# Attention and a low-rank mixer on one core: finer loads and another order for batch 0, narrower unread matmuls, V loaded once, V of batch 1 ahead of the last quarter of w2

## The chip, the core and the metric

The kernel runs on one core of a Trainium2 chip. A core has five engines that run beside each other and meet at semaphores: TensorE (PE: matmuls, and PEld, its loads of weights), VectorE (DVE), ScalarE (ACT), GpSimd (POOL) and SyncE (SP). POOL and SP also issue transfers (DMAs), which 16 DMA engines carry out. SBUF is the working memory of 128 partitions, PSUM the memory that matmuls write. The metric is the time of one execution in microseconds (us) of the device, as the median of several runs. A profile comes from one execution; its "span" is from the first instruction to the last, and the execution's time has some 1.7 us more around it.

## The reference

Sliding-window causal attention (each query sees itself and the 63 positions before it) over 8 batches, 8 heads, 576 positions and 64 elements a head, and after it a mixer: a low-rank mix over the positions (U and V of rank 32) added to the attention's output, then a two-layer MLP with relu, and u added again.

```python
scores = scale * np.matmul(q, k.transpose(0, 1, 3, 2))
rel = pos[:, None] - pos[None, :]
mask = (rel >= 0) & (rel < 64)
scores = np.where(mask, scores, -1e9)
attn = softmax(scores)
x = np.matmul(attn, v)            # to (8, 576, 512)
h = x.transpose(0, 2, 1) @ U @ V
u = x + h.transpose(0, 2, 1)
out = u + np.maximum(u @ w_ch1, 0.0) @ w_ch2
```

All inputs and the output are float32 in memory; the kernel computes in bf16 with float32 sums.

## The kernel before, in words

The order on every engine is the order in which the program's text issues instructions; it is written out by hand.

**Two kinds of work, interleaved.** The MLP runs over 9 chunks of 512 tokens (`mlp(c)`). Each chunk has 32 slots: slots 0 to 15 are one feature tile each of the first layer (`ch1`, line 655: 4 matmuls of 128x512, relu on DVE or ACT), slots 16 to 31 are one token tile and a quarter of the sum each of the second layer (`ch2`, line 678: 4 matmuls of 128x512; after the last quarter DVE adds u, line 687, and SP writes the tile out, line 690). In chunk 0 the second layer goes by pairs of token tiles, quarter by quarter. Attention of batch c+1 is cut into pieces that are put behind certain slots of chunk c, by the tables `PLACE`, `PLACE_0` to `PLACE_3`:

- T: transposes of keys and queries. Batches 0 and 1 use PE (line 274) with a copy from PSUM (`TK` and `TQ`, lines 285 and 290). From batch 2 on SP transposes them by DMA (`TX`, line 296), ten for a batch, at the slots of `CROSS`.
- S: scores of a pair of heads, and the exp on ACT (line 357); a last one (`SC8`, tiles `low` and `high` from batch 2 on) takes the last block of all heads.
- M: the mask, as a product. In batch 0 the mask is added by PE before the scores instead (B, line 327).
- SV: shifted copies of the values (`shift_high`, `shift_low`), from tile `vA` to tile `vB`.
- PV: probabilities times values (line 399), with a division on DVE.
- U, V: the low-rank mix (lines 498 and 506; line 577), and u in bf16 (line 590). For V there is `vrep`, a bf16 copy of the matrix V that stands four times on 32 partitions each.
- UT: u transposed for the MLP (tile `uTc`), by PE (line 609) for batches 0 to 2 and by SP's DMA (line 605) from batch 3 on.

**Batch 0 ahead of everything.** Before chunk 0 there is nothing to interleave with, so batch 0's attention is written out piece by piece in the string `order`. Ahead of it and between its pieces stand matmuls on a tile `idle` whose result nobody reads (`turn_over`, line 749): 56 of 96 columns, and five of 512 columns.

**Transfers.** POOL's queue issues, in this order: keys and queries of batch 0 (heads 0 to 3, then 4 to 7), the values of batch 0 (`load_v(0)`), w1 in two halves, keys and queries of batch 1, w2's first two quarters, the values of batch 1, w2's last two quarters, keys and queries of batch 2. Between them stand POOL's own instructions: masks, and shifted copies that wait for values. A transfer waits for the one issued eight before it. Later, `held` (line 869) makes POOL wait for batch 2's transposes before it loads the values of batch 2 and the keys and queries of batch 3. SP's queue issues U and V, then the transposes and the outputs.

Of the kernel before, what the change touches and what calls it, by code (L numbers as in the profile page):

```python
# [12 lines left out]
FP32 = mybir.dt.float32  # L13
# [3 lines left out]
def kernel(  # L17
# [11 lines left out]
    nc = tc.nc  # L29
    B, H, S, D = q.shape  # L30
    DM = H * D
    R = moe_U.shape[1]
    F = moe_w_ch1.shape[1]
    P = nc.NUM_PARTITIONS
    W = 64
# [3 lines left out]
    NFC = F // P  # L39
# [6 lines left out]
    NFULL = S // P  # L46
    CH = 512
# [18 lines left out]
    ps_tp = ctx.enter_context(tc.tile_pool(name="ps_tp", bufs=1, space=bass.MemoryType.PSUM))  # L66
    first = ExitStack()
    psum = {
        "mm": first.enter_context(tc.tile_pool(name="ps_t0", bufs=2, space=bass.MemoryType.PSUM)),
        "spare": first.enter_context(tc.tile_pool(name="ps_s0", bufs=1, space=bass.MemoryType.PSUM)),  # L70
    }

    ctx.enter_context(tc.manual_schedule())
# [6 lines left out]
    w2b = const.tile([P, NFC, DM], BF16, name="w2b")  # L80
# [1 line left out]
    uf = [const.tile([P, NT, R], FP32, name=f"uf{i}") for i in range(2)]  # L82
    ub = [const.tile([P, NT, R], BF16, name=f"ub{i}") for i in range(2)]
    vrep = const.tile([P, W + S + W], BF16, name="vrep")
    vf = const.tile([P, S], FP32, name="vf")
    idle = const.tile([P, CH], BF16, name="idle")
    xs = [const.tile([P, NT, H, D], BF16, name=f"xs{i}") for i in range(2)]
    vA = [const.tile([P, NFULL, H, VW], BF16, name=f"vA{i}") for i in range(2)]
# [17 lines left out]
    def load_kq(b, split):  # L106
        grouped = b < NGR
        if grouped:
            kb, qb = (
                r[0:GP, :].rearrange("p (h c d) -> p h c d", h=H, c=GR) for r in (kr[b % 2], qr[b % 2])  # L110
            )
        else:
            kb, qb = kn[b % 2], qn[b % 2]
        loaded[b] = (kb, qb)
        if grouped:
            for h0, h1 in ((0, 4), (4, 8)) if split else ((0, H),):
                hs = slice(h0, h1)
                for t, src in ((kb, k), (qb, q)):
                    nc.gpsimd.dma_start(
                        out=t[:, hs, :, :].rearrange("p h c d -> p h (c d)"),  # L120
                        in_=src[b, hs, :, :].rearrange("h (p c) d -> p h (c d)", c=GR),
                    )
                    yield
        else:
            for t in range(NT):
                rows = P if t < NFULL else W
                for dst, src in ((kb, k), (qb, q)):
                    nc.gpsimd.dma_start(  # L128
                        out=dst[0:rows, t, :, :],
                        in_=src[b, :, t * P : t * P + rows, :].rearrange("h p d -> p h d"),  # L130
                    )
                yield

    def load_v(b):
        va, vb = vA[b % 2], vB[b % 2]
        for t in range(NFULL):
            nc.gpsimd.dma_start(  # L137
                out=va[:, t, :, 0:D],
                in_=v[b, :, t * P : (t + 1) * P, :].rearrange("h p d -> p h d"),
            )  # L140
            if t == NFULL - 1:
                nc.gpsimd.dma_start(
                    out=vb[0:W, t, :, 0:D],
                    in_=v[b, :, (t + 1) * P : (t + 1) * P + W, :].rearrange("h p d -> p h d"),
                )
# [10 lines left out]
    def shift_high(b, copy, t):  # L156
        copy(out=vB[b % 2][W:P, t, :, :], in_=vA[b % 2][W:P, t, :, :])

    def shift_low(b, copy, t):
        copy(out=vB[b % 2][0:W, t, :, :], in_=vA[b % 2][0:W, t + 1, :, :])  # L160
# [14 lines left out]
        channel_multiplier=1,  # L175
    )
    nc.vector.memset(maskA[:, 0, 0:2, :], 1.0)
    for _ in kq0:
        pass


    for n, base, step, mult in ((0, 0, 1, -1), (1, -1, -1, 1), (1, W, 1, -1)):
        nc.gpsimd.affine_select(
            out=maskA[:, 0, n, :],
            in_=maskA[:, 0, n, :],
            compare_op=ALU.is_ge,
            fill=0.0,
            base=base,
            pattern=[[step, W]],
            channel_multiplier=mult,  # L190
        )
    for i in range(2):
        nc.vector.memset(vA[i][:, :, :, D:VW], 1.0)
        nc.vector.memset(vB[i][:, :, :, D:VW], 1.0)
# [16 lines left out]


    def load_low_rank():
        for part in (vf[:, 0:1], uf[1][:, 0, :], uf[1][:, 1, 0:1]):
            nc.vector.memset(part, 0.0)
        for g in range(4):
            nc.sync.dma_start(out=vf[g * R : (g + 1) * R, :], in_=moe_V[:, :])
        nc.sync.dma_start(out=uf[1][W:P, 0, :], in_=moe_U[0:W, :])
        nc.sync.dma_start(
            out=uf[1][:, 1:NT, :], in_=moe_U[W:S, :].rearrange("(c p) r -> p c r", p=P)  # L220
        )

    w1v = moe_w_ch1.rearrange("(c p) n -> p c n", p=P)
    for lo, hi in ((0, 1024), (1024, 2048)):
        nc.gpsimd.dma_start(out=w1b[:, :, lo:hi], in_=w1v[:, :, lo:hi])
    for t in range(2):
        shift_high(0, nc.gpsimd.tensor_copy, t)
        shift_low(0, nc.gpsimd.tensor_copy, t)
    shift_low(0, nc.gpsimd.tensor_copy, 2)
    for _ in load_kq(1, False):  # L230
        pass
    w2v = moe_w_ch2.rearrange("(i p) m -> p i m", p=P)
    for i in range(0, NFC, 4):
        if i == NFC // 2:
            load_v(1)
        nc.gpsimd.dma_start(out=w2b[:, i : i + 4, :], in_=w2v[:, i : i + 4, :])

    u_tiles = {}
    uT_tiles = {}
# [7 lines left out]
    def attention(b, spare=False):  # L247
# [14 lines left out]
        def tr(src, j, wide=False):  # L262
            if spare and turn[0] % 3 != 0:
                tpb = psum["mm"].tile([P, 2 * CH], BF16, name="tpm", tag="mm")
                tp = tpb[:, 0:S].rearrange("d (c p) -> d c p", c=GR)
            elif wide:
                tpw = ps_big.tile([P, 2, 2 * CH], BF16, name="tpw", tag="big")
                tp = tpw[:, 0, 0:S].rearrange("d (c p) -> d c p", c=GR)
            else:
                tp = ps_tp.tile([P, GR, GP], BF16, name="tpg", tag="tp")  # L270
            turn[0] += 1
            for c in range(GR):
                for g in range(2):
                    nc.tensor.transpose(  # L274
                        tp[g * D : (g + 1) * D, c, :], src[:, 2 * j + g, c, :], ident[0:GP, 0:GP]
                    )
            return tp.rearrange("d c p -> d p c")

        def place_of(f, j):
            return f[j].rearrange("d (p c) -> d p c", c=GR)  # L280

        def TK(j):
            def f():
                copy = nc.vector.tensor_copy if spare and j == 2 else nc.scalar.copy
                copy(out=place_of(kt, j), in_=tr(kb, j))
            return f

        def TQ(j):
            def f():
                nc.vector.tensor_copy(out=place_of(qt, j), in_=tr(qb, j, b == 1))  # L290
            return f

        def TX(t):
# [237 lines left out]

        def idle_turns(n):
            cols = P if opened else CH
            for _ in range(n * (CH // cols)):
                nc.tensor.matmul(
                    bank(0)[:, 0:cols],
                    idle[:, 0:P],
                    idle[:, 0:cols],
                    start=not opened,
                    stop=not opened,  # L540
                )
# [104 lines left out]
    def mlp(c):  # L646
# [60 lines left out]
    }  # L707
    PLACE_0 = {"V": [0, 0, 1, 2, 2, 3, 4, 4]}
    PLACE_1 = {
        "T": [10, 10, 11, 11, 12, 12, 13, 13],  # L710
        "S": [11, 12, 13, 14, 15],
        "M": [12, 13, 14, 15, 16],
        "SV": [16, 16, 17, 17],
        "PV": [18],
        "U": [23],
        "V": [24, 25, 26],
        "UT": [27, 28, 29, 30, 102],
    }
    PLACE_2 = {
# [12 lines left out]
        "PV": [10],  # L732
        "U": [16],
        "V": [18, 19, 20],
        "UT": [19, 19, 20, 20, 21],
    }
    CROSS = {
        0: {2: [16, 17, 18, 19, 20]},
# [5 lines left out]

    unread = psum["spare"].tile([P, CH], FP32, name="unread", tag="spare")

    def turn_over(n, cols=CH):
        for _ in range(n):
            nc.tensor.matmul(
                unread[:, 0:cols], idle[:, 0:P], idle[:, 0:cols], start=True, stop=True  # L750
            )


    turn_over(56, 96)
    att = {0: attention(0, spare=True)}
    a = att[0]
    nc.vector.tensor_scalar(
# [22 lines left out]
        nc.vector.tensor_copy(out=mask[:, 7, :], in_=mask[:, 1, :])  # L780

    repeat(nc.scalar.copy, maskB)
    order = "K0 K1 B0 B1 Q0 Q1 S0 S1 K2 K3 B2 Q2 B3 Q3 S2 S3 B4 S4"
    for what in order.split():
        j = int(what[1])
        if what[0] in "SB":
            a[what[0]][j]()
        else:
            a["T"][2 * j + (what[0] == "Q")]()
        if what == "Q1":  # L790
            load_low_rank()
        turn_over({"B1": 1, "Q1": 1, "S1": 1, "B2": 1, "Q3": 1}.get(what, 0))
    nc.scalar.copy(out=ub[0][:], in_=uf[0][:])
    for t in range(2, NFULL):
        shift_high(0, nc.scalar.copy, t)
    nc.scalar.copy(out=vrep[:, W : W + S], in_=vf[:])
    for t in range(NT + 2):
        if t < NT:
            a["PV"][t]()
        if 2 <= t < NFULL + 2:  # L800
            a["XT"][t - 2]()
            a["U"][t - 2]()
        elif t == 1:
            a["idle"](1)
    for f in [a["U"][NT - 1]] + a["X3"] + a["HT"]:
        f()
    repeat(nc.vector.tensor_copy, maskA[:, 0])
# [100 lines left out]
```

The softmax here doesn't subtract the row's maximum and nothing guards it: scores larger than these inputs give would overflow.

## Time and profile before

| | us |
|---|---|
| median of 4 runs (lowest to highest) | 318.74 (318.58 to 319.21) |
| the profiled execution | 318.89 |
| its span | 317.2 |
| PE busy | 306.3 |
| DVE busy | 163.0 |
| ACT busy | 109.5 |
| POOL busy | 97.9 |
| first matmul of the MLP starts | 23.43 |
| one 128x512 matmul of the MLP, as listed (they overlap) | 0.379 |
| one exp of a pair of heads, 128x1024 | 1.03 |
| POOL's transfers: packets, MB | 100096, 18.36 |
| SP's transfers: packets, MB | 51744, 20.77 |

A busy time is the union of an engine's instructions. Matmuls are pipelined, so that four of 128x512 take some 0.87 us together although one is listed with 0.379 us. In a list of waits, a line is: who waited, for whom, us in total, how often, the longest. In a list of instructions in order of time a line is: start, us, engine, line, operation, output from inputs, shapes, count, and in brackets the idle time before it with what ended it. In a table by stretches a line is: the stretch, its length, the busy time of PE, PEld, DVE, ACT and POOL with their counts, the granted clock of PE, the share of the DMA engines, and GB/s. The landing of a transfer is given as the time from its issue.

### The profile page before, as it was taken

Reading aid. Unit: us, or ns where it says so; the run is one execution under the profiler, and the core shown is the slowest. Engines: PE = TensorE matmul, PEld = TensorE weight load, DVE = VectorE, ACT = ScalarE, POOL = GpSimd, SP = SyncE. Lnnn points to the kernel's source line nnn. Section 1 sums busy time; section 2 is a strip of 40 time slices with the busy share of each in tenths; the row PEclk is TensorE's granted clock in tenths of the full one; section 3 lists DMA queues with packets and bytes.
Section 4 is the critical chain, followed back from the end, with each engine's and each line's share of the span. In section 5 each row is a group of like instructions: output and inputs, shape, how many; then the busy total and the mean of one; then the engine's idle time right before and its main releaser. Section 6 shows DMA issues by size and latency. Waiting matters only on the chain.

```text
span 317.2 us, 6876 instructions
## 1 busy us (share of the span) xinstructions
PE 306.3 (97%) x2856; PEld 149.2 (47%) x2856; DVE 163.0 (51%) x297; ACT 109.5 (35%) x176; POOL 97.9 (31%) x127
## 2 busy tenths in 40 slices
PE   7889999999998999899999999999999999999995
PEld 6544554544454544354445444544454444444442
DVE  4464558428655955575557455745474443016011
ACT  3555670358126620444034503450345003201500
POOL 8671273169735354442544460000000000000000
PEclk9999999999999999999999999999999999999999
DMA  7999999999999999999999999955100520020011
GB/s 111 159 222 205 187 176 126 138 163 196 125 137 194 156 132 181 172 135 157 159 174 150 166 156 157 172 90 135 66 2 2 129 87 2 23 76 33 2 66 66
DMA packets 151871, 39.56 MB, mean 125 GB/s; under 512 B 140960, under 2 KB 146080, under 8 KB 151840
## 3 DMA queue, kind: packets, MB, share of 16 engines
q0 software_dynamic: 100096, 18.36, 79.5%
q1 hardware_dynamic: 51744, 20.77, 40.7%
q8 instruction: 22, 0.36, 0.5%
q14 instruction: 9, 0.07, 0.1%
HBM read 37.14 MB, written 9.44 MB: 147 GB/s over the span
## 4 chain that ended last, share of the span: by engine, by line
PE 92%; DMA 4%; DVE 1%; issue 1%; ACT 1%; SPq 0%; POOLq 0%
PE psA L655 39%; PE psU L678 38%; PE sc L337 3%; PE psv L577 3%; DMA qf<-qr 3%; PE xw L399 2%; DMA kr<-in_k_dram 2%; PE tpg L274 1%; PE pshh L498 1%; PE sc L327 1%; ACT pts L357 1%; PE tpm L274 1%; PE xr L399 1%; DVE qf L290 0%; DVE osb L687 0%
## 5 line engine op out<-in xcount | busy, mean ns | idle before, releaser
L655 PE MATMUL psA<-uTc,w1b 128*128 128x512 bf16 x576 | 130.9, 379 | 2.0 <-DVE osb L687 1.5
L678 PE MATMUL psU<-w2b,c 128*128 128x512 bf16 x576 | 131.4, 379 | 0.0
L678 PEld LDWEIGHTS <-c 128*128 128x128 bf16 x576 | 55.5, 98 | 65.6 <-issue 0.8
L655 PEld LDWEIGHTS <-w1b 128*128 128x128 bf16 x576 | 54.0, 98 | 66.4 <-issue 3.0
L667 ACT ACTIVATE c<-psA 128x512 bf16<-128x512 f32 x84 | 50.1, 597 | 88.9 <-PE psA L655 87.9
L687 DVE TENSOR_TENSOR osb<-psU,un 128x512 f32<-128x512 f32 x36 | 24.7, 691 | 75.1 <-PE psU L678 74.8
L665 DVE TENSOR_SCALAR c<-psA 128x512 bf16<-128x512 f32 x60 | 41.3, 689 | 28.5 <-PE psA L655 28.5
L590 DVE TENSOR_TENSOR un<-psv,xs 128x512 bf16<-128x512 f32 (+1 forms) x40 | 25.6, 684 | 23.2 <-PE psv L577 23.1
L137 POOL DMA_DIRECT2D vA<-in_v_dram x32 | 28.7, 903 | 18.0 <-DMA w1b<-in_moe_w_ch_dram 4.6
L128 POOL DMA_DIRECT2D kr<-in_k_dram x30 | 25.4, 848 | 27.0 <-DMA vA<-in_v_dram 15.1
L357 ACT ACTIVATE pts<-sc 128x1024 bf16<-128x1024 f32 x32 | 31.4, 1029 | 3.8 <-PE sc L337 3.8
L128 POOL DMA_DIRECT2D qr<-in_q_dram x30 | 25.5, 850 | 21.1 <-DMA vA<-in_v_dram 12.3
L390 ACT ACTIVATE ptl<-low 128x256 bf16<-128x256 f32 x6 | 2.3, 384 | 64.2 <-PE high L337 64.2
L363 DVE TENSOR_TENSOR pts<-pts,maskA 128x1024 bf16<-128x1024 bf16 x28 | 19.1, 681 | 0.1
L466 DVE TENSOR_TENSOR xs<-xw,rcw 128x896 bf16<-128x896 f32 x14 | 15.3, 1091 | 0.5
L337 PEld LDWEIGHTS <-kf 64*64 64x64 bf16 x704 | 10.0, 107 | 9.6 <-issue 9.4
L337 PE MATMUL sc<-qf,kf 64*64 64x128 bf16 (+1 forms) x608 | 12.1, 212 | 1.5 <-issue 0.8
L577 PE MATMUL psv<-hh,vrep 128*128 128x512 bf16 x40 | 12.5, 379 | 0.0
L399 PEld LDWEIGHTS <-pts 128*64 128x64 bf16 x512 | 9.9, 110 | 4.4 <-issue 3.1
L612 ACT COPY uTc<-tpu 128x512 bf16<-128x512 bf16 x9 | 5.3, 586 | 11.5 <-PE tpu L609 11.5
L399 PE MATMUL xw<-vA,pts 128*64 128x65 bf16 x217 | 8.5, 195 | 0.0
L513 ACT CAST hh<-pshh 128x512 bf16<-128x512 f32 x7 | 4.1, 582 | 12.5 <-PE pshh L506 12.5
(107 smaller groups left out, 164.2 us busy)
## 6 DMA issues: line engine op xcount, KB each, us to landing
out_dram<-osb SPq DMA_DIRECT2D x36, 256.0 KB, 5.7
vA<-in_v_dram POOLq DMA_DIRECT2D x32, 128.0 KB, 13.8
kr<-in_k_dram POOLq DMA_DIRECT2D x24, 128.0 KB, 13.3
qr<-in_q_dram POOLq DMA_DIRECT2D x24, 128.0 KB, 12.4
w1b<-in_moe_w_ch_dram POOLq DMA_DIRECT2D x2, 1024.0 KB, 15.2
w2b<-in_moe_w_ch_dram POOLq DMA_DIRECT2D x4, 512.0 KB, 15.1
kr<-in_k_dram POOLq DMA_DIRECT2D x2, 288.0 KB, 6.5
qr<-in_q_dram POOLq DMA_DIRECT2D x2, 288.0 KB, 6.5
```

Source lines behind the costliest of these rows:

```text
L128: nc.gpsimd.dma_start(out=dst[0:rows, t, :, :], in_=src[b, :, t * P : t * P + rows, :].rearrange("h p d -> p h d"),)
L137: nc.gpsimd.dma_start(out=va[:, t, :, 0:D], in_=v[b, :, t * P : (t + 1) * P, :].rearrange("h p d -> p h d"),)
L337: nc.tensor.matmul(sc[g][r0 : r0 + W, col * W : (col + n) * W], keys_of(j, u, rs), queries_of(j, blk, n, rs), start=not spare, stop=last o ...
L357: nc.scalar.activation(out=dst, in_=sc[:], func=ACT.Exp, scale=scale)
L399: nc.tensor.matmul(dst, pts[:, h // 2, h % 2, blk, :] if blk < NB - 1 else ptl[:, h // 2, h % 2, :], rhs, start=True, stop=True,)
L577: nc.tensor.matmul(ps[0][:, n, :], vrep[:, off : off + P], hh["sb"][:], start=True, stop=True)
L590: nc.vector.tensor_tensor(out=u_tiles[g][rs, :], in0=ps[0][rs, n, :], in1=x[rs, t, :, :].rearrange("p h d -> p (h d)"), op=ALU.add,)
L655: nc.tensor.matmul(ps[i][:], w1b[:, dc, i * P : (i + 1) * P], uTc[:, :, dc, :], start=(dc == 0), stop=(dc == NDC - 1),)
L665: nc.vector.tensor_relu(out=c1[i][:], in_=ps[i][:])
L667: nc.scalar.activation(out=c1[i][:], in_=ps[i][:], func=ACT.Relu)
L678: nc.tensor.matmul(acc[t][:], c1[i][:, t * P : (t + 1) * P], w2b[:, i, :], start=(i == 0), stop=(i == NFC - 1),)
L687: nc.vector.tensor_tensor(out=osb[:], in0=acc[t][:], in1=u_tiles[g][:], op=ALU.add)
```

## The change

Batch 0's second half of keys and queries is loaded in two parts of two heads, the last of them behind the masks. The pieces of batch 0 come in another order, the copies of its transposes are dealt out to DVE and ACT anew, and the five unread matmuls of 512 columns go. The 56 unread matmuls of 96 columns become 196 of 32 columns on 32 columns of weights. V is loaded once, to 32 partitions, and spread to `vrep` by four copies, two on POOL and two on ACT. The second copy of U is loaded after batch 0's values. Of the shifted values of batch 0, `shift_high` of tile 1 moves from POOL to ACT, and ACT's stand between the values' pieces. w1 comes in a quarter, a quarter and a half, the half behind POOL's shifts. The values of batch 1 are issued ahead of w2's last quarter instead of ahead of its third. Batch 1's pieces are put one slot later, up to V, and batch 3's UT one slot earlier.

```diff
-            for h0, h1 in ((0, 4), (4, 8)) if split else ((0, H),):
+            for h0, h1 in ((0, 4), (4, 6), (6, 8)) if split else ((0, H),):
...
     nc.vector.memset(maskA[:, 0, 0:2, :], 1.0)
-    for _ in kq0:
-        pass
-
+    next(kq0)
+    next(kq0)
...
+    for _ in kq0:
+        pass
...
     def load_low_rank():
-        for part in (vf[:, 0:1], uf[1][:, 0, :], uf[1][:, 1, 0:1]):
+        nc.vector.memset(vf[:, 0:1], 0.0)
+        nc.sync.dma_start(out=vf[:], in_=moe_V[:, :])
+
+    def load_low_rank_1():
+        for part in (uf[1][:, 0, :], uf[1][:, 1, 0:1]):
             nc.vector.memset(part, 0.0)
-        for g in range(4):
-            nc.sync.dma_start(out=vf[g * R : (g + 1) * R, :], in_=moe_V[:, :])
         nc.sync.dma_start(out=uf[1][W:P, 0, :], in_=moe_U[0:W, :])
...
-    for lo, hi in ((0, 1024), (1024, 2048)):
+    def load_w1(lo, hi):
         nc.gpsimd.dma_start(out=w1b[:, :, lo:hi], in_=w1v[:, :, lo:hi])
-    for t in range(2):
-        shift_high(0, nc.gpsimd.tensor_copy, t)
-        shift_low(0, nc.gpsimd.tensor_copy, t)
-    shift_low(0, nc.gpsimd.tensor_copy, 2)
-    for _ in load_kq(1, False):
-        pass
-    w2v = moe_w_ch2.rearrange("(i p) m -> p i m", p=P)
-    for i in range(0, NFC, 4):
-        if i == NFC // 2:
-            load_v(1)
-        nc.gpsimd.dma_start(out=w2b[:, i : i + 4, :], in_=w2v[:, i : i + 4, :])
+    def spread_v(g, copy):
+        copy(out=vrep[g * R : (g + 1) * R, W : W + S], in_=vf[:])
+
+    def load_rest():
+        load_w1(0, 512)
+        load_w1(512, 1024)
+        shift_high(0, nc.gpsimd.tensor_copy, 0)
+        shift_low(0, nc.gpsimd.tensor_copy, 0)
+        for t in range(1, 3):
+            shift_low(0, nc.gpsimd.tensor_copy, t)
+        load_w1(1024, 2048)
+        for g in range(2):
+            spread_v(g, nc.gpsimd.tensor_copy)
+        for _ in load_kq(1, False):
+            pass
+        w2v = moe_w_ch2.rearrange("(i p) m -> p i m", p=P)
+        for i in range(0, NFC, 4):
+            if i == NFC - 4:
+                load_v(1)
+            nc.gpsimd.dma_start(out=w2b[:, i : i + 4, :], in_=w2v[:, i : i + 4, :])
...
-                copy = nc.vector.tensor_copy if spare and j == 2 else nc.scalar.copy
+                copy = nc.vector.tensor_copy if spare and j >= 2 else nc.scalar.copy
...
-                nc.vector.tensor_copy(out=place_of(qt, j), in_=tr(qb, j, b == 1))
+                copy = nc.scalar.copy if spare and j == 1 else nc.vector.tensor_copy
+                copy(out=place_of(qt, j), in_=tr(qb, j, b == 1))
...
     PLACE_1 = {
-        "T": [10, 10, 11, 11, 12, 12, 13, 13],
-        "S": [11, 12, 13, 14, 15],
-        "M": [12, 13, 14, 15, 16],
-        "SV": [16, 16, 17, 17],
-        "PV": [18],
-        "U": [23],
-        "V": [24, 25, 26],
+        "T": [11, 11, 12, 12, 13, 13, 14, 14],
+        "S": [12, 13, 14, 15, 15],
+        "M": [13, 14, 15, 16, 17],
+        "SV": [17, 17, 18, 18],
+        "PV": [19],
+        "U": [24],
+        "V": [25, 26, 27],
         "UT": [27, 28, 29, 30, 102],
...
         "V": [18, 19, 20],
-        "UT": [19, 19, 20, 20, 21],
+        "UT": [18, 18, 19, 19, 20],
...
-    def turn_over(n, cols=CH):
+    def turn_over(n, cols, rows=P):
         for _ in range(n):
             nc.tensor.matmul(
-                unread[:, 0:cols], idle[:, 0:P], idle[:, 0:cols], start=True, stop=True
+                unread[0:rows, 0:cols], idle[:, 0:rows], idle[:, 0:cols], start=True, stop=True
             )
...
-    turn_over(56, 96)
+    turn_over(196, R, R)
...
-    order = "K0 K1 B0 B1 Q0 Q1 S0 S1 K2 K3 B2 Q2 B3 Q3 S2 S3 B4 S4"
+    order = "K0 K1 B0 B1 Q0 Q1 K2 S0 S1 Q2 B2 K3 S2 Q3 B3 S3 B4 S4"
...
         if what == "Q1":
             load_low_rank()
-        turn_over({"B1": 1, "Q1": 1, "S1": 1, "B2": 1, "Q3": 1}.get(what, 0))
-    nc.scalar.copy(out=ub[0][:], in_=uf[0][:])
-    for t in range(2, NFULL):
-        shift_high(0, nc.scalar.copy, t)
-    nc.scalar.copy(out=vrep[:, W : W + S], in_=vf[:])
+            nc.scalar.copy(out=ub[0][:], in_=uf[0][:])
+    load_rest()
     for t in range(NT + 2):
         if t < NT:
             a["PV"][t]()
+        if t < 3:
+            shift_high(0, nc.scalar.copy, t + 1)
+        elif t < NT:
+            spread_v(t - 1, nc.scalar.copy)
...
+    load_low_rank_1()
```

Two small parts are left out: the order in which two pools of PSUM are made, and one PSUM tile that is taken a little earlier.

## The prediction

> **What bounds the kernel now.** I read the page first (lines 1 and 4), then PE's waits, then the instructions in order of time around each wait, then the landings of the transfers.
>
> The page says that TensorE (PE) is busy for 97% of the span, and the chain that ended last is PE for 92%:
>
> ```profile
> PE 306.3 (97%) x2856; PEld 149.2 (47%) x2856; DVE 163.0 (51%) x297; ACT 109.5 (35%) x176; POOL 97.9 (31%) x127
> PE 92%; DMA 4%; DVE 1%; issue 1%; ACT 1%; SPq 0%; POOLq 0%
> ```
>
> No matmul with a used result is added or removed, so what can change is PE's idle time and its work before the first matmul of the MLP. PE's waits hold all of the idle time that matters:
>
> ```profile
> PE psA L655 <- DVE osb L687: 1.5, 1, 1.5
> PE unread L749 <- DVE idle L164: 1.3, 1, 1.3
> PE low L337 <- DMA qf<-qr: 0.8, 1, 0.8
> PE sc L337 <- issue: 0.8, 2, 0.6
> PE tpg L274 <- DMA kr<-in_k_dram: 0.6, 1, 0.6
> ```
>
> The front ends where PE begins the MLP, at 23.43 us. Two later waits matter as much, 0.80 us at 98.37 us and 1.52 us at 129.65 us:
>
> ```profile
> 23.43 1.89 PE L655 MATMUL psA<-uTc,w1b 128*128 128x512 bf16 x8 [0.44 <-DVE uTc L564]
> 98.37 0.19 PE L337 MATMUL low<-qf,kf 64*64 64x64 bf16 x1 [0.80 <-DMA qf<-qr]
> 129.65 1.02 PE L655 MATMUL psA<-uTc,w1b 128*128 128x512 bf16 x4 [1.52 <-DVE osb L687]
> ```
>
> The first of these two says that PE is not the bound up to 98 us: a chain of transfers is. Followed back: that matmul needs batch 3's last query transpose, issued by SP at 89.91 us, landed 8.3 us later. SP's ten transposes for batch 3 began at 75.01 us, when batch 3's first keys had landed (issued at 69.71 us, 5.2 us on the way). POOL could issue those only after its `held` copy at 69.19 us, which waits for batch 2's last query transpose. Batch 2's ten transposes began at 50.48 us, right after batch 2's first keys landed (39.65 + 10.7 = 50.35 us), behind the last quarter of w2 (36.40 + 13.3 = 49.7 us). Before that POOL's transfers land one after the other without a hole: w1's halves at 9.46 + 13.0 = 22.5 and 10.2 + 17.4 = 27.6 us.
>
> ```profile
> 39.65 0.90 POOL L128 DMA_DIRECT2D kr<-in_k_dram  x1 [2.51 <-PE sc L337]
> 50.48 1.30 SPq L296 DMA_TRANSPOSE kf<-kr  x1
> 69.19 0.18 POOL L869 COPY held<-qf 1x1 bf16<-1x1 bf16 x1 [2.20 <-DMA qf<-qr]
> 69.71 0.89 POOL L128 DMA_DIRECT2D kr<-in_k_dram  x1 [0.34 <-issue]
> 75.01 1.20 SPq L296 DMA_TRANSPOSE kf<-kr  x1
> 89.91 1.45 SPq L296 DMA_TRANSPOSE qf<-qr  x1
> ```
>
> No link of this chain waits for work that the front makes earlier. So what the front gains on PE is given back at 98 us, unless the chain of transfers is shortened too.
>
> **The change part by part.**
>
> *Exps back to back (new order, finer loads of batch 0).* In the profile the exps come in two pairs, ending at 11.82 and 16.23 us, with 2.4 us between them for batch 0's other keys and queries. Loads land in order: keys 0 to 3 at 6.22, queries 0 to 3 at 7.7, keys 4 to 7 at 9.7, queries 4 to 7 at 11.3 us. Cut in two, heads 4 and 5 come about half way: keys near 8.6, queries near 9.5; heads 6 and 7 at 10.4 and 11.3. With the row prices (copy 0.64 on ACT, 0.76 on DVE, cast of U 0.33, scores 0.35, mask 0.5, exp 1.0 each): Q1's copy on ACT 8.8 to 9.4 and the cast to 9.7; exp 0 9.85 to 10.85; exp 1 to 11.8; Q2's copy ends at 11.25, scores 2 at 12.1, exp 2 to 13.1; Q3's copy ends at 13.25, scores 3 at 13.65, exp 3 to 14.65 instead of 16.22. That is 1.55 us. The values follow with the rows' pitch (0.84 us, set by DVE); the third needs a shift on POOL that waits for V's last tile (issued at 7.92, landed 9.0 later, at 16.9, plus a copy of 0.62 gives 17.6), 0 to 0.6 us later than my order asks. Front gain on PE: 1.0 to 1.55 us, I take 1.4. The five 512-wide unread matmuls lay in waits and are part of it. ACT's shifts and spreads (five copies after the last exp) end near 19, before the cast of hh near 20.1.
>
> *196 unread matmuls of 32 columns for 56 of 96.* Before: 4.39 us for 56, 78 ns each, 0.81 ns a column, ending at 5.65, with 0.61 us to spare. At that price per column one of 32 takes 26 ns: 196 take 5.1 us and end at 6.4, beside the landing at 6.22: 0.1 us late at most, inside my 1.4. Bounds: 18 score pairs in 0.35 us (20 ns each, so 3.9 us) and 78 ns if the pair and not the column has the price (15.3 us). I take the column, as the nearest row is the same instruction.
>
> [...] The row of before shows 78 ns for a pair whose load alone is listed at about 98 ns in the MLP, so there they overlapped.
>
> *V loaded once.* Three of four 72 KB loads go. w1's halves land 5.1 us apart for 1024 KB, 200 KB a us, so 216 KB cost the chain at most 1.1 us; nothing if they ran beside it. The bandwidth was 247 GB/s while they ran and 216 after them, so they were partly free:
>
> ```profile
> 17.00:18.00 1.00, 0.70 (x26) 0.39 (x20) 0.96 (x3) 1.00 (x2) 1.00 (x2) 1.00 1.15 247
> 24.00:25.00 1.00, 1.00 (x7) 0.45 (x5) 0.40 (x3) 0.00 (x0) 0.00 (x0) 1.00 1.18 216
> ```
>
> I take 0.55 us. The spread costs two copies on POOL (no row; nearest 0.62 us for 64x520, so 1.3 us) ahead of batch 1's keys, and w1's second half now waits behind a shift until 17.6. Both are hidden: w1's first half still fills the queue until about 22, and these were issued 12 us ahead of their landing. If that cover went, the chain would lose what is missing. U's shifted load moves to about 21 us, at the same price.
>
> *w1 in three, V1 ahead of w2's last quarter.* Same bytes up to batch 2's first keys, so 0 for the chain. V1 lands one w2 quarter later (512 KB, 2.5 us): near 46.2 instead of 44.7. Values of batch 1 are due at 46.69 + 0.87 (one slot later) - 1.4 = 46.2, and the last shift ends near 47: 0 to 0.9 us of PE's gain is lost there. w2's last quarter lands at 49.7 - 0.55 = 49.1 and is needed three slots of 0.87 after 47.98, less 1.4, at 49.2: nothing. POOL, SP: four more transfers of 0.7 us, two of them ahead of V, which starts 1.2 us later, behind a queue that is full until 11.3 us.
>
> *At 98 us.* PE comes at 97.57 - 1.4 + (0 to 0.9), 96.2 to 97.1; the transpose lands at 98.2 - 0.55 = 97.7. Gain there: 0.55 us; the rest of PE's gain becomes a longer wait.
>
> *Batch 3's UT one slot earlier.* The wait at 129.65 is put down to DVE's osb, which was done; the late one is SP's third transpose for chunk 3, issued at 121.43 and landed 8.1 us later, at 129.55. SP was held at 116.07 by the output of tile 0, which waits for osb until 118.3:
>
> ```profile
> 116.07 2.59 SPq L690 DMA_DIRECT2D out_dram<-osb  x2
> 118.71 2.62 SPq L605 DMA_TRANSPOSE uTc<-un  x2
> 121.43 5.75 SPq L605 DMA_TRANSPOSE uTc<-un  x3
> 116.30 1.40 DVE L590 TENSOR_TENSOR un<-psv,xs 64x512 bf16<-64x512 f32 x2 [3.89 <-PE psv L577]
> ```
>
> Now two transposes go first, from 117.0 (un's first tile), then the output near 119.6, then the third at 120.2: 1.25 us earlier. Bounds: 0, if SP's queue lands at a fixed pace whatever the issue, and 1.5, the whole wait. I take 1.25: the two outputs before them were issued 2.25 us apart and landed 2.4 us apart, so SP's hole passes through to the landings.
>
> **Sum.** 0.55 + 1.25 = 1.8 us. The profiled execution took 318.89 us, 317.2 of span and 1.7 around it; it would become 317.1. The median of the runs is 318.74, 0.15 below it: 316.9 us. Own range, with 0 to 1.1 and 0.9 to 1.5: gains of 0.9 to 2.6, so 316.1 to 317.8.
>
> **Rivals.** Differences under 0.2% (0.64 us) cannot be told from no change; the runs before span that much.
>
> 1. *The chain of transfers gains more* (V's one load at the full 1.1 us, and V0's slow tiles, 2.0 and 1.6 us apart against 1.1, lose 0.5 of their excess as nothing runs beside them): 1.6 + 1.25 = 2.85, 315.9 us. Against it: V1's tiles show the same uneven pace with no V load near. 12%.
> 2. *The transposes keep their landings,* as SP's queue is some 8 us deep: 0.55 alone, 318.2 us. For it: the five transposes landed 7.1 to 8.5 us after their issue, about the depth of six of them. 16%.
> 3. *Slower: the unread matmuls outlast the load.* They stand ahead of everything on PE. The front then comes later by 196 p - 5.0 us, for a pair price p, less 1.4. PE's 0.8 us of spare at 98 us and the 1.25 us later cover a lateness of 2.05 us; over 2.7 the kernel is slower by over 0.2%, that is from p = 46 ns on. If load and matmul each cost 26 ns, p = 52: 5.2 - 1.4 - 2.05 = 1.75 us slower, 320.5 us; at 78 ns 325.6. Against it: the price per column. 12%.
> 4. *The chain of transfers is longer,* as POOL's copies or waits leave a hole in it: at 2.5 us (one w2 quarter) 2.5 - 1.25 = 1.3 us slower, 320.0 us. 6%.
>
> My forecast has the remaining 54%. Faster by over 0.2%: all of it but 2, all of rival 1 and 5 of rival 2: 69%. Same: 11 and 2 and 1 of the slower ones: 14%. Slower: 17%. The range leaves out the slower rivals and the far end of rival 1: 315.6 to 319.2 us.
>
> **What would show it.** The last exp of batch 0's pairs ends near 14.7; the first MLP matmul starts near 22.0; the unread ones end near 6.4 at 26 ns. w1's last part lands about 0.5 us earlier than 27.6. PE's wait for qf before `low` in chunk 2 grows from 0.8 to between 0.6 and 1.6 us and ends near 97.8. The wait at chunk 3's start falls from 1.5 to about 0.3. I am wrong if that wait at 98 us is gone and the gain is the front's, or if the first key transpose starts after 8 us.

## The result, and the profile after

The changed kernel takes 320.74 us (median; 317.90 to 323.24), the kernel before 318.58 in the runs beside it: a ratio of 1.0059, with a 95% interval of 1.0047 to 1.0071. By this ratio it is 1.9 us slower, by the medians 2.2 us, where a gain of 1.8 us was forecast. Two of its 44 runs, over 1.5% above its fastest, are left out of the ratio and of the counts below. Its profiled execution took 321.8 us, 320.1 of them span.

Its lines are numbered some 15 higher than those of the kernel before. Its page, lines 1 (busy us, share, count), 2 (granted clock in 40 slices of 8.0 us) and 4 (the chain that ended last):

```profile
PE 310.5 (97%) x2991; PEld 152.6 (48%) x2991; DVE 162.4 (51%) x297; ACT 110.9 (35%) x178; POOL 100.1 (31%) x131
PEclk9659999999999999999999999999999999999999
PE 91%; DVE 3%; DMA 3%; issue 1%; ACT 1%; SPq 0%
```

PE is busy for 4.2 us more than before, and the clock row has a hole: 0.6 and 0.5 of full speed in the second and third slices, which is the front. PE's waits of the changed kernel:

```profile
PE sc L342 <- issue: 1.6, 1, 1.6
PE psA L671 <- DMA uTc<-un: 1.3, 1, 1.3
PE unread L765 <- DVE idle L164: 1.3, 1, 1.3
PE sc L352 <- issue: 0.5, 1, 0.5
```

The wait for `qf` at 98 us is gone. A new one leads the list, and it is for nothing that the profile shows ("issue"). Its place, in the instructions of PE in order of time:

```profile
1.26 5.39 PE L765 MATMUL unread<-idle 128*32 128x32 bf16 x196 [1.26 <-DVE idle L164]
6.58 0.45 PE L288 MATMUL tpg<-ident,kr 96*64 96x96 bf16 x12
...
7.21 0.82 PE L342 MATMUL sc<-maskB,ident 128*128 128x512 bf16 x3
9.59 0.42 PE L342 MATMUL sc<-maskB,ident 128*128 128x512 bf16 x1 [1.56 <-issue]
9.95 0.69 PE L288 MATMUL tpm<-ident,qr 96*64 96x96 bf16 x12
...
27.23 1.89 PE L671 MATMUL psA<-uTc,w1b 128*128 128x512 bf16 x8 [0.44 <-DVE uTc L580]
...
132.37 1.02 PE L671 MATMUL psA<-uTc,w1b 128*128 128x512 bf16 x4 [1.33 <-DMA uTc<-un]
```

The unread matmuls end at 6.65 us. After the first transposes PE stands for 1.56 us between the third and the fourth of four equal mask matmuls, whose operands are there. Behind it twelve transposes take 0.69 us instead of 0.45: the clock. The MLP begins at 27.23 us, 3.8 later than before. This time as a table by stretches, of the changed kernel, and then the two middle stretches of the kernel before (the sixth number behind the stretch's length is the clock):

```profile
5.00:10.00 5.00, 3.44 (x93) 2.48 (x91) 0.70 (x3) 1.58 (x3) 4.96 (x7) 0.98 1.33 191
10.00:15.00 5.00, 4.92 (x107) 3.65 (x110) 2.31 (x5) 2.80 (x4) 3.42 (x5) 0.50 2.35 147
15.00:20.00 5.00, 4.77 (x101) 3.08 (x97) 1.97 (x4) 3.29 (x5) 3.61 (x6) 0.50 1.29 204
20.00:25.00 5.00, 4.94 (x57) 2.60 (x57) 3.91 (x11) 2.29 (x4) 5.00 (x7) 0.66 1.11 201
```

```profile
10.00:15.00 5.00, 4.57 (x109) 2.66 (x108) 2.35 (x7) 3.13 (x4) 2.85 (x5) 1.00 2.43 146
15.00:20.00 5.00, 4.17 (x111) 2.73 (x100) 3.11 (x8) 3.34 (x7) 3.62 (x6) 1.00 1.22 216
```

From 9.79 to 23.44 us the granted clock is 0.50, which the profile of the kernel before does not show there. This execution lost more of its clock than most: its mean clock is 0.979, which 6 of 42 runs have or fall below, while 24 lie between 0.986 and 0.989, about half as much lost (an estimate from the means). Later waits give some back: 3.8 us late at the front, less the 0.80 us of wait that fell away at 98 us and the 0.2 us by which the wait at chunk 3 shrank, is 2.8 us; the span is 2.9 us longer.

So there were two things to explain: what PE waited for, and whether the lost clock is its consequence. Theory A: the wait is for PE's own instructions, since 196 pairs of weight load and matmul pass in 5.4 us; the gap then costs the clock. Theory B: the five wide unread matmuls ("fillers"), taken out by the change, had kept the clock up. Theory C: the narrow matmuls themselves (only 32 rows and columns) do not keep it up.

### The profile page after: what moved, and what is told of

It reads as the page before. It is cut to its first block, busy times and chain, and to the rows that moved or that the text cites. A ratio compares the mean times of both kernels' runs of the same rounds, so it can differ in the third digit from the quotient of the medians.

```text
span 320.1 us, 7144 instructions
## 1 busy us (share of the span) xinstructions
PE 310.5 (97%) x2991; PEld 152.6 (48%) x2991; DVE 162.4 (51%) x297; ACT 110.9 (35%) x178; POOL 100.1 (31%) x131
## 4 chain that ended last, share of the span: by engine, by line
PE 91%; DVE 3%; DMA 3%; issue 1%; ACT 1%; SPq 0%
PE psA L671 40%; PE psU L694 34%; PE sc L352 3%; DMA uTc<-un 3%; PE psv L593 3%; PE xw L414 2%; PE unread L765 2%; PE sc L342 1%; PE tpg L288 1%; DVE un L606 1%; PE xr L414 1%; DVE xs L481 1%; ACT pts L372 1%; PE tpu L625 1%; DVE osb L703 1%
## 5 line engine op out<-in xcount | busy, mean ns | idle before, releaser
L128 POOL DMA_DIRECT2D kr<-in_k_dram x30 | 25.5, 850 | 25.1 <-DMA vA<-in_v_dram 12.8
L414 PEld LDWEIGHTS <-pts 128*64 128x64 bf16 x512 | 10.7, 116 | 4.4 <-issue 3.2
```

What stands on the lines that cost most here:

```text
L128: nc.gpsimd.dma_start(out=dst[0:rows, t, :, :], in_=src[b, :, t * P : t * P + rows, :].rearrange("h p d -> p h d"),)
L414: nc.tensor.matmul(dst, pts[:, h // 2, h % 2, blk, :] if blk < NB - 1 else ptl[:, h // 2, h % 2, :], rhs, start=True, stop=True,)
```

## The experiments

**Wide unread matmuls back (e1, and again as e11).** The whole change stays, but for the unread matmuls ahead of the front:

```
-    turn_over(196, R, R)
+    turn_over(56, 96)
```

> The changed kernel with the 56 unread matmuls of 96 columns of before in place of its 196 of 32; the five of 512 columns stay out. Theory A (the number of instructions ahead of the first transposes: PE runs dry of instructions 1.56 us in front of the fourth mask matmul, and the clock falls after that gap): no such gap, clock 1.00 from 10 to 23 us, first MLP matmul near 22, no wait at 98 us or a short one, 316.3 to 317.3 us. Theory B (the clock fell because the five wide unread matmuls between batch 0's pieces went): clock 0.50 in 10 to 23 us as in the changed kernel, first MLP matmul after 25 us, 319 us or more.

> The changed kernel with 56 unread matmuls of 96 columns once more, on the chip of the other two, as their reference: 316.3 to 317.3 us, clock 1.00 from 10 to 23 us.

Measured: 316.87 us, ratio 0.9922 (0.9893 to 0.9951), and again 316.79, ratio 0.9937 (0.9905 to 0.9969). PE of e1 in order of time:

```profile
6.08 0.45 PE L288 MATMUL tpg<-ident,kr 96*64 96x96 bf16 x12 [1.00 <-DMA kr<-in_k_dram]
...
14.64 0.45 PE L414 MATMUL xr<-vA,pts 128*64 128x65 bf16 x16 [0.55 <-ACT pts L372]
...
16.73 0.19 PE L414 MATMUL xr<-vB,pts 128*64 128x65 bf16 x1 [1.15 <-POOL vB L160]
...
22.32 1.89 PE L671 MATMUL psA<-uTc,w1b 128*128 128x512 bf16 x8 [0.44 <-DVE uTc L580]
...
47.04 0.22 PE L414 MATMUL xw<-vB,pts 128*64 128x65 bf16 x1 [0.74 <-DVE vB L160]
...
97.07 0.19 PE L352 MATMUL low<-qf,kf 64*64 64x64 bf16 x1 [0.31 <-DMA qf<-qr]
...
127.19 1.02 PE L671 MATMUL psA<-uTc,w1b 128*128 128x512 bf16 x4 [0.35 <-DMA uTc<-un]
```

No gap for issue in the front, the clock at 0.999, the MLP from 22.32 us. This one line of the change holds the whole loss; the rest of the change makes the kernel 2.0 to 2.4 us faster (against the runs of the kernel before beside them, 319.22 and 318.82). Part of that is the clock, as the kernel before loses some of it too: 31 of its 83 runs beside the experiments have a mean clock of at most 0.995, against 1 of the 18 of e1 and e11. Among the runs with at least 0.996 the medians are 318.32 us (52 runs of before) and 316.65 us (17 of e1 and e11), 1.7 us apart. The result speaks against B, as there are no fillers between the pieces here, but A and C both pass.

**The five wide fillers back beside the 196 (e2).** 

```
+        turn_over({"B1": 1, "Q1": 1, "S1": 1, "B2": 1, "Q3": 1}.get(what, 0), CH)
```

> The changed kernel with the five unread matmuls of 512 columns put back behind B1, Q1, S1, B2 and Q3, the 196 narrow ones kept. Theory A: the gap of about 1.5 us stays, in front of the same instruction, and the clock falls again, so 320 to 322 us. Theory B: the clock stays at 1.00 through the gap, about 318.5 us.

Measured: 319.90 us, ratio 1.0019 (0.9990 to 1.0048). The gap is still in front of a mask matmul (1.33 us, ending at 9.60), and a second one stands at 15.80 us (0.98 us). The mean clock of the ten runs is 0.989 to 1.0, higher than the changed kernel's, where 36 of 42 had at most 0.989. In the profiled execution (0.999) neither gap was followed by a loss. So the fillers seem to help to hold the clock, and do nothing against the gap. B is part of the clock's story at most.

**Only the narrow matmuls, in the kernel before (e3).**

```
-    turn_over(56, 96)
+    turn_over(196, R, R)
...
```

(Left out: `turn_over` takes the number of rows, as in the change.)

> The kernel before with the 196 narrow unread matmuls in place of its 56 of 96 columns, nothing else. Theory A: a gap of about 1.5 us in front of the fourth mask matmul and a clock of 0.50 behind it, 321 to 324 us. Theory B: the five wide ones keep the clock, only the gap counts, 319.5 to 320.5 us. If the narrow ones cost nothing: 318.6 us.

Measured: 321.34 us, ratio 1.0080 (1.0042 to 1.0117). PE of e3 in order of time:

```profile
1.25 5.28 PE L749 MATMUL unread<-idle 128*32 128x32 bf16 x196 [1.25 <-DVE idle L164]
...
9.60 0.38 PE L327 MATMUL sc<-maskB,ident 128*128 128x512 bf16 x1 [1.68 <-issue]
```

The same gap before the last mask matmul of the group, in the old order and with the old loads. The clock stayed at 1.00 to 11.2 us, with the narrow matmuls long over, and was 0.50 from some 11.4 to 18.2 us. This profile is of the slowest of the six runs (mean clock 0.983); five of them have a mean clock of at most 0.995. The narrow matmuls alone bring the gap and, in most runs, the lost clock, and the fillers, which this kernel has, did not prevent it.

**Fewer and wider ones in two sizes (e4, e5).** 

```
e4   turn_over(12, CH)
e5   turn_over(98, 2 * R, 2 * R)
```

> The changed kernel with 12 unread matmuls of 512 columns in place of 196 of 32: the same columns, 24 instructions instead of 392. Theory A: no gap, the clock stays, 316.3 to 317.3 us like the run with 56 of 96. Theory B: clock 0.50 in 10 to 23 us, 319 us or more.

> The changed kernel with 98 unread matmuls of 64 columns for 196 of 32: the same columns, 196 instructions fewer. If the gap belongs to a place in PE's instructions (the 449th after its first branch), it moves 196 instructions on, to the end of the transposes of keys 6 and 7, which run some 4 us later: no gap in front of the fourth mask matmul, at most 0.5 us in front of the scores behind those transposes, clock 1.00, 316.3 to 317.5 us. If the gap belongs to the mask matmuls or to narrow unread ones as such, it stays where it was, 319 us or more.

Measured: e4 316.49 us, ratio 0.9909 (0.9879 to 0.9939); e5 316.12 us, ratio 0.9914 (0.9883 to 0.9945). PE of e5 in order of time:

```profile
1.26 4.41 PE L765 MATMUL unread<-idle 128*64 128x64 bf16 x98 [1.26 <-DVE idle L164]
6.16 0.45 PE L288 MATMUL tpg<-ident,kr 96*64 96x96 bf16 x12 [0.48 <-DMA kr<-in_k_dram]
...
18.80 0.19 PE L414 MATMUL xr<-vA,pts 128*64 128x65 bf16 x1 [0.63 <-issue]
...
23.33 1.89 PE L671 MATMUL psA<-uTc,w1b 128*128 128x512 bf16 x8 [0.44 <-DVE uTc L580]
```

Half the number of pairs, still small ones of 64 rows and columns: no gap for issue ahead of 9 us, and the clock at 1.00. A gap for issue of 0.63 us turns up later, at 18.80. The MLP begins 1.0 us later than in e1, but from there on e5 has no wait over 0.15 us. 196 pairs of 32 columns and 98 of 64 have the same 6272 columns, so what the gap of 1.56 us went with is the number of instructions. e5 has the lowest median of all versions and beats both kernels; e1, e4 and e5 cannot be told apart by their intervals.

**16 pairs fewer (e9).** If PE runs out at a fixed place in its list of instructions, the gap must move by 16 matmuls, out of the mask matmuls.

```
-    turn_over(196, R, R)
+    turn_over(180, R, R)
```

> The changed kernel with 180 unread matmuls of 32 columns for 196, 32 instructions fewer. If PE runs dry at a fixed place in its instructions, the gap is in front of the instruction that stands 32 further on in the text: the fourth transpose of queries 2 and 3, after three of them have run, 1.0 to 1.6 us long, and the clock falls in some executions: 319 to 321 us. If the gap is bound to the mask matmuls or to a time: it is in front of the fourth mask matmul again.

Measured: 318.23 us, ratio 0.9981 (0.9946 to 1.0017). PE of e9 in order of time:

```profile
8.52 0.25 PE L288 MATMUL tpg<-ident,qr 96*64 96x96 bf16 x3
9.05 0.37 PE L288 MATMUL tpg<-ident,qr 96*64 96x96 bf16 x9 [0.28 <-issue]
...
14.98 0.25 PE L352 MATMUL sc<-qf,kf 64*64 64x128 bf16 x5 [0.74 <-issue]
```

The place is as expected: one mask matmul, twelve transposes and three more, 16 matmuls further on. Its length is a miss: 0.28 us instead of 1.0 to 1.6, and the time stays under the 319 us that went with it. A second gap stands 9 + 12 + 36 + 12 + 2 + 12 + 18 + 12 + 2 + 13 = 128 matmuls behind the first. Counting the matmuls that the traces list ahead of the gaps for issue gives the same two places in kernel after kernel (a few records are missing, so a count can be one or two short):

| kernel | unread ahead | matmuls ahead of the 1st gap | its us | ahead of the 2nd | its us |
|---|---|---|---|---|---|
| before | 56 | 223 | 0.18 | - | - |
| changed | 196 | 223 | 1.56 | - | - |
| e2 | 196 | 222 | 1.33 | 349 | 0.98 |
| e3 | 196 | 222 | 1.68 | - | - |
| e4 | 12 | 222 | 0.18 | - | - |
| e5 | 98 | - | - | 350 | 0.63 |
| e7 (below) | 56 | 223 | 0.25 | - | - |
| e9 | 180 | 223 | 0.28 | 351 | 0.74 |

Not every wait for issue lies on these places: e3 has one of 0.39 us at 338. The kernel before shows the first place too, in front of a score matmul, and a longer wait later on:

```profile
14.77 0.38 PE L337 MATMUL sc<-qf,kf 64*64 64x128 bf16 x14 [0.18 <-issue]
...
43.77 0.22 PE L337 MATMUL sc<-qf,kf 64*64 64x64 bf16 x4 [0.60 <-issue]
```

The longer one has 605 matmuls ahead of it, as have those of e10 (0.62 us) and e6 (0.64); the changed kernel's 0.48 us at 47.19 us has 733, one period of 128 more. From 223 to 605, and from 351 to 733, are 382 matmuls, three periods less two.

The pages list as many weight loads as matmuls, so 128 matmuls are 256 instructions. The transfers show a queue "instruction" with one transfer of 16384 bytes at a time. That it is PE's is an estimate that fits its number of transfers: 22 before and 23 in the changed kernel, where 2856 and 2991 loads and as many matmuls make 22.3 and 23.4 times 256. Its line in the transfers of 11.5 to 12.9 us of the kernel before, and then of 7.2 to 8.2 us of the changed one (queue, packets, MB, share of one stretch of 16 engines):

```profile
q8 instruction: 1, 0.02, 5.6%
```

```profile
q8 instruction: 1, 0.02, 5.9%
```

It begins at 11.55 us before and at 7.24 us in the changed kernel, 4.3 us earlier, and 2.4 us ahead of the end of the gap; in e9 it begins at 6.81, 2.2 us ahead of the end of its gap. So the place, the period of 128 matmuls and the transfer together read as PE's instructions coming in blocks of 256, and PE waiting where it reaches a block before it is there: the first half of theory A. Which instructions a transfer brings, no view shows. Why e9's first gap is 1.28 us shorter than the changed kernel's can be read off as well: PE reached the place 0.73 us later (8.77 against 8.04 us), and the gap ended 0.54 us earlier, as the transfer began 0.43 us earlier. From the end of the transfer to the end of the gap it is 1.3 to 2.0 us in the two kernels' waits for issue (from 12.80 to 14.77 and from 42.12 to 43.77 us before, from 8.19 to 9.59 and from 45.90 to 47.19 in the changed kernel). What decides how early a transfer begins stays open.

**The gap without the narrow matmuls (e6).** Is the lost clock the gap's consequence? In e1 the mask was made late by two unneeded fills on DVE, so that PE waits in front of the same group of mask matmuls, for the mask and not for its instructions:

```
+    nc.vector.memset(pts[:], 0.0)
+    nc.vector.memset(ptl[:], 0.0)
```

> The run with 56 unread matmuls of 96 columns, with two clears on DVE ahead of the mask, so that PE waits some 1.6 us in front of the first mask matmul with all its instructions at hand. If a gap of this length is what takes the clock: a clock of 0.50 behind it in most executions, mean clock below 0.995 there, 319 to 321 us. If the clock fell for the narrow unread matmuls: it stays at 1.00 and only the gap counts, 317 to 318.5 us.

Measured: 318.92 us, ratio 1.0003 (0.9972 to 1.0033), 2.1 us over e1. PE of e6 in order of time, and then its table by short stretches:

```profile
8.72 1.20 PE L342 MATMUL sc<-maskB,ident 128*128 128x512 bf16 x4 [1.80 <-ACT maskB L794]
```

```profile
9.00:9.40 0.40, 0.40 (x4) 0.12 (x2) 0.00 (x0) 0.40 (x2) 0.40 (x2) 1.00 1.30 200
9.50:9.90 0.40, 0.40 (x4) 0.06 (x4) 0.00 (x0) 0.24 (x1) 0.40 (x2) 0.50 1.70 171
12.40:12.80 0.40, 0.40 (x16) 0.38 (x12) 0.00 (x0) 0.40 (x1) 0.38 (x1) 0.50 2.31 147
12.90:13.30 0.40, 0.26 (x7) 0.20 (x4) 0.18 (x1) 0.40 (x2) 0.40 (x1) 1.00 2.58 150
```

A gap of 1.80 us behind wide unread matmuls is followed by half the clock from some 9.4 to 12.8 us. So here a gap was enough, without a narrow matmul. That the narrow ones have no part in it (theory C) is not shown: the changed kernel loses its clock more often behind a shorter gap (36 of 42 runs with at most 0.989, against 5 of 12 here). The mean clock of its twelve runs is between 0.970 and 1.0, and eight have at most 0.995, so the loss comes in most executions, and with different lengths.

**UT back to its old slots, in e1 (e7).** 

```
-        "UT": [18, 18, 19, 19, 20],
+        "UT": [19, 19, 20, 20, 21],
```

> The run with 56 unread matmuls of 96 columns, with batch 3's UT at its old slots. If the earlier slots are worth what the prediction says, the wait at the start of chunk 3 is 1.2 us longer than with them and the time 1.0 to 1.3 us longer, near 318.0 us. If SP's transposes land at a fixed pace: no difference, 316.9 us.

Measured: 317.56 us, ratio 0.9968 (0.9935 to 1.0001); 0.7 us more than e1. PE of e7 at the start of chunk 3, to be set beside 0.35 us in e1 and 1.02 us in e11:

```profile
127.82 1.02 PE L671 MATMUL psA<-uTc,w1b 128*128 128x512 bf16 x4 [1.53 <-DMA uTc<-un]
```

That the earlier slot shortens the wait is not shown: with it, the profiles of e8 and e10, which keep this part of the change too, have 0.61 and 1.29 us there, and that of e4 2.28 us, more than e7. The intervals of the times overlap as well.

**V loaded four times, in e1 (e8).** 

```
-        nc.sync.dma_start(out=vf[:], in_=moe_V[:, :])
+        for g in range(4):
+            nc.sync.dma_start(out=vf[g * R : (g + 1) * R, :], in_=moe_V[:, :])
...
```

(Left out: the tile `vf` gets 128 partitions, and each copy reads its own 32.)

> The run with 56 unread matmuls of 96 columns, with V loaded four times to 128 partitions as before and spread from there. If the three loads cost the chain of transfers 0.55 us, w1's last part lands 0.5 us later than with one load, near 27.5 us, and the wait at 98 us ends 0.5 us later: 317.2 to 317.5 us. If they run beside it: the same landing within 0.2 us and 316.9 us.

Measured: 317.39 us, ratio 0.9940 (0.9915 to 0.9964); 0.5 us more than e1, which is within the intervals. w1's last part landed at 28.06 us instead of 27.07 (26.69 in e11 and 27.28 in e10, with one load too), and PE of e8 waits longer in chunk 2:

```profile
97.69 0.19 PE L353 MATMUL low<-qf,kf 64*64 64x64 bf16 x1 [1.23 <-DMA qf<-qr]
```

The three loads cost the chain of transfers 1.0 to 1.4 us at w1's landing. At 98 us that is 0.9 us more wait, with PE 0.3 us earlier than in e1.

**V1 back ahead of w2's third quarter, in e1 (e10).** 

```
-            if i == NFC - 4:
+            if i == NFC // 2:
```

> The run with 56 unread matmuls of 96 columns, with the values of batch 1 issued ahead of w2's third quarter as before. By the prediction the order is worth nothing for the chain of transfers (batch 2's first keys land within 0.3 us of where they did), and the wait for batch 1's shifted values (0.74 us in the run with the new order) goes; PE's time there is spare: the same time within 0.3 us. If the new order is worth something: 317.3 us or more.

Measured: 317.40 us, ratio 0.9946 (0.9919 to 0.9974), against 316.79 and 0.9937 (0.9905 to 0.9969) of e11 beside it. Inconclusive: the first keys of batch 2 landed at 49.28 us against 48.88 in e11 and 49.57 in e1, and the 0.74 us of wait for shifted values that e1 has near 47 us is not there in e10, nor in e11. Whether this order is worth anything is not settled.

## Why the prediction was wrong

**The step that failed** is the one on the 196 unread matmuls: "196 take 5.1 us and end at 6.4, beside the landing at 6.22: 0.1 us late at most, inside my 1.4." The price was right: 5.39 us for 196 is 27.5 ns each, against 26 by the column. Both were taken mostly ahead of the first clock record of their traces, a 1.00 from 5.22 us on before and from 6.38 us on in the changed kernel: in the kernel before the unread matmuls start 80 ns apart ahead of 5.2 us, and 42 to 43 ns apart behind it; in the changed kernel all but the last few start ahead of 6.38 us, from the second on 26 to 28 ns apart. What was left out is their number. The step bounded what an instruction costs PE when it runs, and not what it costs to have it there. The kernel before had the sign of it in view, a wait for issue of 0.18 us 223 matmuls into the program. With 140 more matmuls ahead, that place is reached at 8.0 us instead of 14.6, and PE waits there for 1.56 us, by the reading above for a block that is not in yet. A second thing was put at nothing: "what can change is PE's idle time and its work before the first matmul of the MLP" leaves out the clock, which in the profiled execution was 0.50 for 13.65 us behind the gap, in the front itself.

**What came in its place.** At the medians, the forecast missed by 3.8 us. The two of the changed kernel's 42 runs whose mean clock was 0.999 or 1.0 took 318.67 and 318.55 us, 1.7 over e1: that would be the gap. The median lies 2.1 us higher still: that would be the clock. Two runs carry this division, and the fastest of all (317.90 us) had 0.992, so it is an estimate. Rival 3 had the sign and nearly the time (320.5 us), but not the mechanism: it has the unread matmuls outlast the load of the keys by 4.1 us or more (its 2.7 us, and the 1.4 us of the front's gain). They ended at 6.65, and the first key transposes stand at 6.58 against 6.08 in e1, 0.5 us late.

**The other steps,** as far as e1 and e11 show them without the narrow matmuls:

- *Exps back to back:* right. The values begin at 14.64 us instead of 16.27, 1.6 earlier (forecast 1.55). The MLP begins at 22.32 and 22.46, where 22.0 was forecast: a gain of 1.0 to 1.1 us, at the low bound of 1.0 to 1.55. The third values wait for POOL's shift for 1.15 and 0.78 us, where 0 to 0.6 was allowed.
- *V loaded once:* 0.55 us was taken, with 1.1 as the upper bound. The time of e8 showed 0.5, not clear of noise, the landing of w1 1.0 to 1.4, about the upper bound. Against the kernel before (27.58 us) w1 landed 0.5 and 0.9 us earlier in e1 and e11, where 0.5 was forecast.
- *The order of V1 and w2:* the forecast 0 for the chain cannot be told from e10. The wait for V1's values was 0.74 us and none, inside 0 to 0.9.
- *At 98 us:* the chain of transfers gained more than I took. A wait of 0.6 to 1.6 us, ending at 97.7, was forecast; it was 0.31 us ending at 97.07 in e1, and none in e11 and e5. This is the direction of rival 1.
- *UT one slot earlier:* not settled. 1.25 us was taken. Beside e7's 1.53 us the wait was 0.35 and 1.02 us in e1 and e11, but 1.29 in e10 and 2.28 in e4, and 1.33 us of it are left in the changed kernel itself; the time of e7 is 0.7 us over e1, within the intervals.
- *The sign of being wrong* came half true: the wait at 98 us was gone, but not because the gain was the front's, as it was put. PE was late, and the transpose had landed at 94.65 us.

With these errors of both signs the sum held where its one bad term was taken out: forecast 316.9 us, e1 316.87 and e11 316.79. That is partly luck: the chain gained more than was taken, what UT gave is not known, and the front gave the low bound. Part of what e1 and e11 gained is clock that the kernel before lost in some of its runs, which the forecast did not hold.

## What to carry to other kernels

Price unread matmuls by their number as well as by their columns: near the start, a few wide ones (12 of 512 columns, 5.3 us, or 98 of 64, 4.4 us) keep PE busy nearly as long as 196 narrow ones (5.4 us), and their first waits for issue were 0.18 us at 16.27 us (e4) and 0.63 us at 18.80 us (e5) instead of 1.56 us at 9.59. Count the matmuls ahead of a wait for "issue": if the count is the same in other kernels, the wait is a place in the list of instructions. Then ask whether an edit makes an engine reach that place sooner. A gap of 1.6 us can cost more than itself, if the clock falls behind it: the changed kernel's median is 3.9 us over e1's, and 36 of its 42 runs have a mean clock of at most 0.989.

## What the runs showed of the hardware

**PE waits for issue at the same counts of matmuls.** These waits stand at 222 to 223 matmuls in seven kernels and at 349 to 351 in three, whatever the matmuls are. That 256 instructions come together there is an estimate from the period of 128 matmuls with a load each and from the 22 and 23 transfers of the queue. The waits' lengths are 0.18 to 1.68 us; from the changed kernel to e9 1.56 us became 0.28, as PE got there 0.73 us later and the transfer began 0.43 us earlier.

**A gap of 1.6 us can cost the clock, and not in every execution.** Half the clock was granted for 13.65 us in the changed kernel (9.79 to 23.44, behind a gap of 1.56 us), for some 3.4 in e6 (behind 1.80 us) and for some 6.8 in e9 (17.5 to 24.3, with gaps for issue of 0.28 and 0.74 us ahead of it). The clock records of the kernel before and of the changed one hold 1.00 and 0.50 and nothing between. Most executions of the two lost some clock: 36 of 42 of the changed kernel have a mean clock of at most 0.989, 8 of 12 of e6 at most 0.995. A gap of 1.15 us in e1, at 15.6 us, was not followed by a loss (mean clock 0.999), nor was one of 2.28 us in e4, at 126.2 us (0.997); e9 lost some of its clock in seven of ten runs (mean clock 0.984 to 0.994).

The records also show how long a clock lasted. In the kernel before it is 1.00 for 310.61 us, from 5.22 to 315.83; in the changed kernel it is 1.00 for 3.41 us (6.38 to 9.79), 0.50 for 13.65 and 1.00 for 296.96 (23.44 to 320.40). These are 91, 1, 4 and 87 times 3.41 us, and the some 3.4 and 6.8 us of e6 and e9 are near one and two times. The changed kernel's gap, 8.04 to 9.59 us, lies whole in the stretch from 6.38 to 9.79, at whose end the clock was halved; e6's gap ended at 8.72, some 0.7 us ahead of its halving. Why a kernel loses its clock in some executions alone is not shown. The length of a gap does not decide it alone: in the profiled executions 1.33 us in e2 (mean clock 0.999) and 1.15 us in e1 were not followed by a loss, 0.74 us in e9 was. What else decides, such as how little PE did around the gap, was not tried and stays open.
